# Attention, gated layer and cosine layer on one core: a planner that holds VectorE's and GpSimd's common port as a resource, and the last queries scaled by the step that reads their scores

## The chip, the cores and the metric

One core of a Trainium2 chip. The time is the device time of one execution in microseconds (us); three runs of the kernel before gave 1183.61, 1184.83 and 1186.10, median 1184.83. The engines are TensorE (PE, with PEld for its weight loads), VectorE (DVE), ScalarE (ACT), GpSimd (POOL) and SyncE (SP, which only issues transfers). Each runs its own list of instructions in order.

## The reference

For 4 batches x 8 heads x 576 tokens x 64, then two dense layers on the 2304 tokens:

```
scores = q @ k^T / 8;  thresh = max(scores) - tau
attn   = exp(scores - max) where scores >= thresh, else 0;  attn /= sum(attn)
x      = attn @ v                             # 2304 x 512
xn     = x / sqrt(mean(x*x) + 1e-6) * rms_g
x      = (silu(xn @ w_gate) * (xn @ w_val)) @ w_out       # 512 -> 1536 -> 512
h      = x @ w_in;  out = (h * cos(h)) @ w_out2           # 512 -> 2048 -> 512
```

## The kernel before

Attention works on 16 pairs of heads (4 batches x 4). The 576 queries of a pair make five score steps: four of 128 queries for both heads (`s`), and one (`s4`) that holds the last 64 queries of both heads. A score step writes one PSUM bank pair per head (`s0`, `s1`; `s4` writes only `s0`). For each step then: VectorE takes the maximum and copies the scores out of PSUM (`max`, L505), which frees the bank; ScalarE takes the exponential (`exp`, L523); GpSimd works out the threshold (`th`, L514); VectorE masks and sums (`mask`, L533); TensorE transposes the result (`t`, tile pst, L573, and the rest columns `c0`, `c1`, tile psc); ScalarE copies that out (`raw`). The two halves of a pair end in a product with v (`av0`, `av1`, tile po, L610), copied out by ScalarE (`avo`, L620). GpSimd divides the pair (`div`, L627), squares it (`sq`, L637) and adds it up over the batch (`x_add`, L641); at the batch's end TensorE sums over the partitions (`xsum`, tile pss, L650), and VectorE, GpSimd and SP turn that into the norm's factors in DRAM (`mean`, `rms`, `rs_out`).

The signs are turned: q is multiplied by -1/8 (`qscale`), so that the maximum becomes a minimum. For the 512 main queries ScalarE does it on its copy (L451). For the last 64 queries, tile q4, GpSimd does it in place before they are transposed (`scale_q4`, L424), 16 times.

The order of all this is written out by a planner (`Plan`). Every step has an engine, a cost and a place from the table `STEPS`: (engine, ns, place in ns, and for transfers the landing). `order()` plays the engines against each other: at each turn it takes the step that can start first, ties going to the lower place, and holds buffers, dependences, and a switch cost on TensorE. The result is only the order in which the instructions are written; on the chip the engines run by semaphores. `WARM_S` puts idle matmuls between the first score steps.

At the end of attention the planner also mixes in the first four units of the gated layer (`gv`, tile pgv, two halves of 12 matmuls each, on chunks 0 and 1 of the tokens). Behind the plan the dense layers run in a fixed order: first the second product of unit 0 (tile px), then the next gv.

The weights come as pairs of 32 bit words; VectorE, ScalarE and GpSimd turn them into floats and split these into a high and a low part (`j1`, `j2`, `j_a`, `j_p`, L281 to L300).

Of the kernel before, what the change touches and what calls it, by code (L numbers as in the profile page):

```python
# [14 lines left out]
ALU = mybir.AluOpType  # L15
# [10 lines left out]

UNIT = 3500
STEPS = {
    "none": ("", 0, 29644),
    "load_k": ("SP", 1700, -153470, 5000),  # L30
    "load_q": ("SP", 1700, 5248, 7000),
    "load_v": ("SP", 1700, 40101, 5000),
    "q4": ("POOL", 850, -97525),
    "pb": ("PE", 440, -11192),
    "pa": ("PE", 440, -25434),
    "pc": ("PE", 330, -13826),
    "pb_a": ("ACT", 590, 96411),
    "pa_a": ("ACT", 690, -507361),
    "pc_a": ("ACT", 480, 51091),
    "s": ("PE", 960, -101976),  # L40
    "s4": ("PE", 490, -10556),
    "warm": ("PE", 640, 138604),
    "max": ("DVE", 830, -168581),
    "exp": ("ACT", 785, 23446),
    "th": ("POOL", 450, -62469),
    "mask": ("DVE", 1040, 14956),
    "t": ("PE", 445, 36814),
    "raw": ("ACT", 595, -118822),
    "c0": ("PE", 220, -2475),
    "c1": ("PE", 440, -168991),  # L50
    "c_raw": ("ACT", 415, 220222),
    "radd": ("POOL", 300, 21216),
    "rinv": ("DVE", 400, -48222),
    "r_out": ("SP", 2100, -37205, 2500),
    "r_in": ("SP", 1700, -118771, 11000),
    "av0": ("PE", 2110, -332350),
    "av1": ("PE", 2660, -226081),
    "avo": ("ACT", 420, -105583),
    "div": ("POOL", 1420, 77077),
    "xout": ("SP", 500, -100632, 2500),  # L60
    "sq": ("POOL", 1200, -21513),
    "x_add": ("POOL", 1420, 100483),
    "xsum": ("PE", 1150, 59463),
    "mean": ("DVE", 150, -541635),
    "rms": ("POOL", 1330, 96684),
    "rs_out": ("SP", 2500, -200342, 2500),
    "x_load": ("SP", 500, 109454, 6000),
    "x_p": ("POOL", 1000, 80792),
    "x_a": ("ACT", 610, -82732),
    "x_d": ("DVE", 610, 41961),  # L70
    "jdma": ("SP", 500, 112560, 5000),
    "j1": ("DVE", 600, -13279),
    "j2": ("DVE", 690, -118552),
    "j_p": ("POOL", 1300, 206161),
    "j_a": ("ACT", 620, 63782),
    "gv": ("PE", 2100, 27390),
    "silu": ("ACT", 500, -78353),
    "hmul": ("DVE", 560, -166673),
    "hhi": ("ACT", 520, -75740),
    "hlo": ("DVE", 720, -172389),  # L80
}
SIGNAL = 100
SWITCH = 100
TILING = {"s": 1, "s4": 3, "av0": 2, "av1": 2}
WARM = (8, 2, 0, 0)
WARM_S = (3, 3, 3, 3, 3, 3)
# [9 lines left out]
class Plan:  # L96
# [19 lines left out]
    def order(self):  # L116
        steps, users = self.steps, dict(self.users)
        missing = [len(s["after"]) for s in steps]
        follow = [[] for _ in steps]
        for s in steps:  # L120
            for x in s["after"]:
                follow[x["n"]].append(s["n"])
        taken, parked = {tag: [] for tag in self.bufs}, {}
        ready = [0] * len(steps)
        freed = {}
        clock = {s["eng"]: 0 for s in steps}
        here = {eng: [] for eng in clock}
        for s in steps:
            if not s["after"]:
                here[s["eng"]].append(s["n"])  # L130
        out = []
        tiling = 0
        while len(out) < len(steps):
            best = None
            for eng, ns in here.items():
                for n in list(ns):
                    s = steps[n]
                    held = [taken[tag][-self.bufs[tag]] for tag, _ in s["take"]
                            if len(taken[tag]) >= self.bufs[tag]]
                    wait = [key for key in held if users.get(key, 1)]  # L140
                    if wait:
                        parked.setdefault(wait[0], []).append(n)
                        ns.remove(n)
                        continue
                    t = max([ready[n], clock[eng]] + [freed[key] for key in held])
                    if eng == "PE" and TILING.get(s["kind"], 0) != tiling:
                        t = max(t, clock[eng] + SWITCH)
                    if best is None or (t, s["place"], n) < best:
                        best = t, s["place"], n
            assert best, "no step can start"  # L150
            t, _, n = best
            s = steps[n]
            eng = s["eng"]
            if eng == "PE":
                tiling = TILING.get(s["kind"], 0)
            here[eng].remove(n)
            for tag, key in s["take"]:
                taken[tag].append(key)
            end = t + s["ns"]
            if eng:  # L160
                clock[eng] = end
            seen = end + s["landing"]
            for key in s["free"]:
                users[key] -= 1
                freed[key] = max(freed.get(key, 0), seen)
                if not users[key]:
                    for x in parked.pop(key, ()):
                        here[steps[x]["eng"]].append(x)
            for x in follow[n]:
                missing[x] -= 1  # L170
                ready[x] = max(ready[x], end if steps[x]["eng"] == eng != "SP" else seen)
                if not missing[x]:
                    here[steps[x]["eng"]].append(x)
            s["t"] = t
            out.append(s)
        return out

    def run(self):
        for s in self.order():
            s["fn"]()  # L180


@with_exitstack
def attention_moe_cos_kernel(
# [16 lines left out]
    nc = tc.nc  # L201
# [38 lines left out]
    qscale = const.tile([P, 1], F32, name="qscale")  # L240
# [96 lines left out]
    q4 = [acst.tile([P, P], F32, name=f"q4{i}") for i in range(2)]  # L337
# [21 lines left out]
    nat, qk, un, hf, pr, xb, rm, sq, pre = {}, {}, {}, {}, {}, {}, {}, {}, {}  # L359
# [60 lines left out]
    def k4_t(ps, p):  # L420
        nc.tensor.transpose(ps, nat["k", p][1].rearrange("p h d -> p (h d)"), ident)

    def scale_q4(p):
        nc.gpsimd.tensor_scalar(q4[p % 2][0:64], q4[p % 2][0:64], qscale[0:64, 0:1], None, op0=ALU.mult)  # L424

    def prep_pe(p, kind):


# [67 lines left out]
    def s_max(n, hd):  # L496

        g = group_of(n)
        if g not in grp:
            grp[g] = {"m": sm_p.tile([P, 5], F32, tag="m", name="m"), "n": 0}  # L500
        ci = grp[g]["n"]
        grp[g]["n"] += 1
        un[n]["ci", hd] = ci
        s = s_p.tile([P, S], F32, tag="s", name="s")
        nc.vector.tensor_scalar(  # L505
            s.rearrange("p (c n) -> p c n", c=2), un[n].pop(("ps", hd))[:, :, 0:288], 1.0, None,
            op0=ALU.mult, op1=ALU.min, accum_out=grp[g]["m"][:, ci:ci + 1],
        )
        un[n]["s", hd] = s
# [263 lines left out]
    def attention():  # L773
# [6 lines left out]
        add = plan.add  # L780
# [1 line left out]

        load_k(0)
        load_q(0)
        scale_q4(0)
        warm(WARM[0])
        for kind, m in zip("bac", WARM[1:]):
            prep_pe(0, kind)
# [4 lines left out]
        smm, mx, ex, mk, thr, sums, done = {}, {}, {}, {}, {}, {}, {}  # L793
        lk, lq, lv = {}, {}, {}
# [5 lines left out]
        for p in range(NPAIRS):  # L800
            n = 5 * p
            if p:
                lk[p] = add("load_k", n, load_k, p, take=[("kn", ("kn", p))])
                lq[p] = add("load_q", n, load_q, p, take=[("qn", ("qn", p)), ("q4", ("q4", p))]
                )
            lv[p] = add("load_v", n, load_v, p, take=[("vn", ("vn", p))])
            if p:
                z = add("q4", n, scale_q4, p, after=[lq.get(p)])
                last = []
                for kind, after, free in (  # L810
                    ("b", [lk.get(p)], [("kn", p)]),
                    ("a", [lq.get(p)], [("qn", p)]),
                    ("c", [lk.get(p), z], [("kn", p), ("q4", p)]),
                ):
                    nm = "q" if kind == "a" else "k"
                    x = add("p" + kind, n, prep_pe, p, kind, after=after + last, free=free,
                        take=[("t", ("pre", p, kind))]
                        + ([] if kind == "c" else [(nm, (nm, p))]),
                    )
                    last = [x]  # L820
                    ready[p].append(add("p" + kind + "_a", n, prep_act, p, kind, after=[x],
                        free=[("pre", p, kind)],
                    ))
        for n in range(NU):
            p, u = divmod(n, 5)
# [18 lines left out]
            if u == g[1][-1]:  # L844
                thr[g] = add("th", n, s_thr, g,
                    after=[mx[x] for x in mx if group_of(x[0]) == g],
# [11 lines left out]
        for j in range(2 * NPAIRS):  # L858
            p, par = divmod(j, 2)
# [124 lines left out]
        for n in range(N_EARLY):  # L984
            c = seq[n][1]
# [5 lines left out]
            x = add("hmul", NU + n, h_mul, n, after=[x, y], free=[("gv", n)])  # L991
            x = add("hhi", NU + n, h_hi, n, after=[x])
            hs.append(add("hlo", NU + n, h_lo, n, after=[x], free=[("hh", n)]))
        plan.run()

    with tc.manual_schedule():
        jobs += [
# [65 lines left out]
        done = 0  # L1063
# [178 lines left out]
```

## Time and profile before

| | |
|---|---|
| time, median of 3 runs | 1184.83 us (1183.61 to 1186.10) |
| the profiled execution | 1183.16 us, span 1181.4 us |
| granted TensorE clock | 0.999 of full |
| attention, with the first units of the gated layer | to 326 us of the span |
| gated layer | to about 780 us |
| cosine layer | to the end |
| busy over the span | PE 98%, DVE 69%, ACT 55%, POOL 29% |

The span runs from the first to the last instruction; 1.8 us of the time lie around it. The end of a matmul is modelled, so that a busy TensorE may still hold small waits; a step's true length is read from its start to the next one's start.

### The profile page before, as it was taken

What the parts mean: (1) busy time and instruction counts of PE and PEld (TensorE: products, weight loads), DVE (VectorE), ACT (ScalarE), POOL (GpSimd) and SP (SyncE); (2) the same over time, 40 slices, a digit from 0 to 9 for tenths busy, and PEclk for the clock granted to TensorE, in tenths of its full rate; (3) what the DMA queues carried; (4) which work ended last, traced back from release to release, by engine and by line L of the source; (5) the groups of instructions that cost most, each with busy time, mean ns of one, the idle gap of its engine ahead of it and who ended that gap; (6) DMA issues with size and microseconds to landing.
All of it is one profiled execution on the core that took longest, in us unless ns stands there. A gap on an engine that the chain in (4) does not pass through costs nothing.

```text
span 1181.4 us, 18229 instructions
## 1 busy us (share of the span) xinstructions
PE 1159.4 (98%) x6832; PEld 1017.9 (86%) x6832; DVE 820.8 (69%) x1571; ACT 647.2 (55%) x1210; POOL 342.3 (29%) x315
## 2 busy tenths in 40 slices
PE   8999999999999999999999999999999999999997
PEld 6666666666889999999999999999999999999995
DVE  5898888898659463644726429578687796867765
ACT  5887777877434221312313215377677676766663
POOL 2344444443744020110201102014234243332222
PEclk9999999999999999999999999999999999999999
DMA  5554323311452030110301102002112021000014
GB/s 123 131 132 112 100 58 78 95 48 46 151 175 76 32 108 1 54 54 1 107 1 50 59 1 83 25 1 72 37 36 72 1 72 36 23 15 1 1 54 108
DMA packets 99449, 71.67 MB, mean 61 GB/s; under 512 B 65040, under 2 KB 89360, under 8 KB 99360
## 3 DMA queue, kind: packets, MB, share of 16 engines
q1 hardware_dynamic: 98256, 70.20, 20.9%
q8 instruction: 54, 0.88, 0.3%
q10 hardware_dynamic: 1040, 0.26, 0.1%
q14 instruction: 35, 0.29, 0.1%
q0 software_dynamic: 64, 0.03, 0.0%
HBM read 60.95 MB, written 9.52 MB: 60 GB/s over the span
## 4 chain that ended last, share of the span: by engine, by line
PE 88%; DVE 3%; issue 3%; DMA 2%; ACT 2%; POOL 1%; SPq 0%; POOLq 0%; DVEq 0%; ACTq 0%
PE pgv L716 23%; PE ph L716 16%; PE po L716 16%; PE px L716 11%; PE s L485 7%; PE po L610 6%; PE pst L573 5%; PE psc L592 1%; PE psa L416 1%; DVE wtmp L286 1%; DVE s L505 1%; DMA raw<-in_moe_w_val_dram 1%; DVE e L533 0%; PE warm L682 0%; PE psb L416 0%
## 5 line engine op out<-in xcount | busy, mean ns | idle before, releaser
L290 POOL TENSOR_TENSOR wtmp<-wtmp,raw 128x512 int32<-128x512 int32 x68 | 96.1, 1413 | 353.3 <-DVE wtmp L286 345.2
L716 PE MATMUL pgv<-xh,whi 128*128 128x384 f32 x576 | 194.0, 337 | 0.0
L716 PE MATMUL pgv<-xl,whi 128*128 128x384 f32 x576 | 193.7, 336 | 0.0
L716 PE MATMUL pgv<-xh,wlo 128*128 128x384 f32 x576 | 193.5, 336 | 0.0
L1147 POOL TENSOR_TENSOR hlo<-r,hhi 128x384 fp32r<-128x384 f32 x96 | 98.0, 1021 | 304.0 <-ACT hhi L1146 248.0
L740 ACT ACTIVATE hh<-pgv 128x384 f32<-128x384 f32 x72 | 35.4, 492 | 254.2 <-PE pgv L716 254.1
L744 DVE TENSOR_TENSOR hh<-hh,pgv 128x384 f32<-128x384 f32 x72 | 39.7, 552 | 164.8 <-ACT hh L740 164.6
L505 DVE TENSOR_SCALAR_CACHE_REDUCE s<-s 128x576 f32<-128x576 f32 x144 | 103.8, 753 | 37.9 <-PE s L485 37.6
L716 PE MATMUL ph<-xh,whi 128*128 128x384 f32 x384 | 129.6, 337 | 0.0
L716 PE MATMUL ph<-xl,whi 128*128 128x384 f32 x384 | 129.5, 337 | 0.0
L716 PE MATMUL ph<-xh,wlo 128*128 128x384 f32 x384 | 129.2, 336 | 0.0
L533 DVE SCALAR_TENSOR_TENSOR e<-s,th,e 128x576 f32<-128x576 f32 x128 | 120.4, 971 | 0.4 <-POOL th L514 0.4
L1129 ACT ACTIVATE t<-ph,magic 128x384 f32<-128x384 f32 x96 | 55.8, 582 | 111.5 <-PE ph L716 111.5
L716 PE MATMUL po<-whi,hlo 128*128 128x512 f32 x288 | 114.5, 398 | 1.4 <-POOL hlo L1147 1.4
L716 PE MATMUL po<-whi,hhi 128*128 128x512 f32 x288 | 113.8, 395 | 0.2 <-ACT hhi L1146 0.2
L716 PE MATMUL po<-wlo,hhi 128*128 128x512 f32 x288 | 113.4, 394 | 0.0
L716 PEld LDWEIGHTS pgv<-xh,whi 128*128 128x128 f32 x576 | 108.2, 188 | 0.5 <-issue 0.5
L716 PEld LDWEIGHTS pgv<-xl,whi 128*128 128x128 f32 x576 | 108.2, 188 | 0.4 <-DVE xl L710 0.3
L716 PEld LDWEIGHTS pgv<-xh,wlo 128*128 128x128 f32 x576 | 108.2, 188 | 0.0
L523 ACT ACTIVATE e<-s,m 128x576 f32<-128x576 f32 x128 | 96.6, 781 | 12.5 <-DVE s L505 12.0
L716 PE MATMUL px<-hhi,whi 128*128 128x384 f32 x288 | 98.2, 341 | 4.0 <-DVE acc L1044 3.6
L1136 DVE SCALAR_TENSOR_TENSOR r<-t,r 128x384 f32<-128x384 f32 x96 | 99.1, 1032 | 3.3
(117 smaller groups left out, 2470.3 us busy)
## 6 DMA issues: line engine op xcount, KB each, us to landing
raw<-in_moe_w_out_dram SPq DMA_DIRECT2D x28, 512.0 KB
raw<-in_moe_w_in_dram SPq DMA_DIRECT2D x16, 512.0 KB
raw<-in_moe_w_gate_dram SPq DMA_DIRECT2D x12, 512.0 KB
raw<-in_moe_w_val_dram SPq DMA_DIRECT2D x12, 512.0 KB
x<-xb SPq DMA_DIRECT2D x16, 288.0 KB
kn<-in_k_dram SPq DMA_DIRECT2D x16, 256.0 KB
vn<-in_v_dram SPq DMA_DIRECT2D x16, 256.0 KB
qn<-in_q_dram SPq DMA_DIRECT2D x15, 256.0 KB
```

The costliest lines, as they stand in the source:

```text
L290: nc.gpsimd.tensor_tensor(tmp, tmp, lw, op=ALU.add)
L485: nc.tensor.matmul(ps[:, c, 0:288], lhs, kh[r, k0:k0 + 288], start=True, stop=True,)
L505: nc.vector.tensor_scalar(s.rearrange("p (c n) -> p c n", c=2), un[n].pop(("ps", hd))[:, :, 0:288], 1.0, None, op0=ALU.mult, op1=ALU.min, ...
L523: nc.scalar.activation(un[n]["e"][:, hd], un[n]["s", hd], AF.Exp, bias=grp[group_of(n)]["m"][:, c], scale=-1.0)
L533: nc.vector.scalar_tensor_tensor(e, un[n].pop(("s", hd)), grp[group_of(n)]["th"][:, ci:ci + 1], e, op0=ALU.is_le, op1=ALU.mult, accum_out= ...
L573: nc.tensor.transpose(ps[:, c], e[:, hd, k0:k0 + P], ident)
L610: nc.tensor.matmul(po[64 * hd:64 * hd + 64, :], vn[:, c, hd, :] if c < 4 else vl[:, hd, :], hf[j]["et"][:, hd, c, :] if c < 4 else hf[j][" ...
L716: nc.tensor.matmul(ps, w[a], x[bb], start=first and i == 0, stop=last and i == 2)
L744: nc.vector.tensor_tensor(hq[n], hq[n], pgv.pop(n)[:, 1, 0:TC], op=ALU.mult)
L1129: nc.scalar.activation(t, ph, AF.Identity, bias=magic[:, 0:1], scale=INV2PI)
L1136: nc.vector.scalar_tensor_tensor(r, t, -C2, r, op0=ALU.mult, op1=ALU.add)
L1147: nc.gpsimd.tensor_tensor(lo, r, f(hi), op=ALU.subtract)
```

## The change

The table gets other costs and other places for every step. The planner gets a set `LOCK` of step kinds of VectorE and GpSimd that use the port: none of them starts in the plan while another of them runs, whichever of the two engines it is on. `BEHIND`, the kinds that would also get a real wait for VectorE's step, is empty, so that no wait is written. `scale_q4` is gone, and the maximum of an `s4` step multiplies by `qscale` instead of 1.0.

```diff
-    "q4": ("POOL", 850, -97525),
-    "s": ("PE", 960, -101976),
-    "s4": ("PE", 490, -10556),
+    "s": ("PE", 960, -21325),
+    "s4": ("PE", 490, 85459),
...
-    "th": ("POOL", 450, -62469),
-    "mask": ("DVE", 1040, 14956),
+    "th": ("POOL", 300, -18608),
+    "mask": ("DVE", 890, -37373),
...
-    "av1": ("PE", 2660, -226081),
+    "av1": ("PE", 2660, -60188),
...
+LOCK = {
+    "mask", "j1", "j2", "x_d", "hlo", "th", "div", "sq", "x_add", "rms", "radd", "x_p", "j_p",
+}
+BEHIND = set()
...
+                    if s["kind"] in LOCK:
+                        t = max(t, port)
...
+            if s["kind"] in LOCK:
+                port = end
+                if eng == "DVE":
+                    holder = s
+                elif s["kind"] in BEHIND:
+                    s["behind"] = holder
...
-    def scale_q4(p):
-        nc.gpsimd.tensor_scalar(q4[p % 2][0:64], q4[p % 2][0:64], qscale[0:64, 0:1], None, op0=ALU.mult)
...
-            s.rearrange("p (c n) -> p c n", c=2), un[n].pop(("ps", hd))[:, :, 0:288], 1.0, None,
+            s.rearrange("p (c n) -> p c n", c=2), un[n].pop(("ps", hd))[:, :, 0:288],
+            qscale[:, 0:1] if n % 5 == 4 else 1.0, None,
...
-            if p:
-                z = add("q4", n, scale_q4, p, after=[lq.get(p)])
...
-                    ("c", [lk.get(p), z], [("kn", p), ("q4", p)]),
+                    ("c", [lk.get(p), lq.get(p)], [("kn", p), ("q4", p)]),
```

**Place 1: TensorE at the end of attention.** Before, the last two products with v (po) of the last pair are followed by gated-layer matmuls (pgv); these are the last rows of po:

```order
L573 MATMUL pst<-ident,el 128x128 x4
L610 MATMUL po<-et,vn 64x256 x8
L610 MATMUL po<-ec,v_96 64x256 x2
L610 MATMUL po<-et,vn 64x320 x8
L610 MATMUL po<-ec,v_96 64x320 x2
L716 MATMUL pgv<-xh,whi 128x384
```

Between them and the sum over the partitions (pss) stand four halves of pgv, 48 matmuls. Now the last rows before the second product (px) of the gated layer are these:

```order
L736 MATMUL pgv<-xl,whi 128x384
L736 MATMUL pgv<-xh,wlo 128x384
L630 MATMUL po<-et,vn 64x320 x8
L630 MATMUL po<-ec,v_96 64x320 x2
L670 MATMUL pss<-ones,sq 128x1 x5
L736 MATMUL px_4139<-hhi,whi 128x384
```

All eight halves of pgv have moved ahead of the last po, and pss stands directly behind it.

**Place 2: TensorE around the last queries' score step of the twelfth pair** (s with `64x288` is s4, s with `128x288` a full step). Before:

```order
L573 MATMUL pst<-ident,e 128x128 x4
L416 MATMUL psa<-ident,qn 128x128 x4
L573 MATMUL pst<-ident,e 128x128 x4
L485 MATMUL s_2891<-k 64x288 x4
L416 MATMUL psc<-ident,kn 128x128
L421 MATMUL psc<-ident,k_2382 128x128
```

Now:

```order
L617 MATMUL psc<-ident,el 64x128
L593 MATMUL pst<-ident,el 128x128 x4
L593 MATMUL pst<-ident,e 128x128 x4
L504 MATMUL s_2913<-k 64x288 x4
L504 MATMUL s_2927<-k,q 128x288
L504 MATMUL s_2928<-k,q 128x288
```

The next full score step has moved directly behind s4. In the whole order a score step stands directly behind a score step in five places now and in three before.

**Place 3: VectorE at the end of attention.** Before, from the maximum of the last pair's s4 on (s,m is max; e and el with sum are masks, el of an s4 step):

```order
L505 TENSOR_SCALAR s,m<-s_3788 128x576
L533 SCALAR_TENSOR_TENSOR e,sum<-s,th,e 128x576 x4
L533 SCALAR_TENSOR_TENSOR el,sum<-s,th,el 128x576
L545 RECIPROCAL r_147<-r_147 128x9
L546 STREAM_TRANSPOSE rt<-r_147 128x32
```

Now:

```order
L524 TENSOR_SCALAR s,m<-s_3716,qscale 128x576
L553 SCALAR_TENSOR_TENSOR e,sum<-s,th,e 128x576 x8
L565 RECIPROCAL r_146<-r_146 128x9
L566 STREAM_TRANSPOSE rt<-r_146 128x32
L730 SCALAR_TENSOR_TENSOR xl<-x_2526,g_sb,xh 128x384
L553 SCALAR_TENSOR_TENSOR el,sum<-s,th,el 128x576
```

Nine masks of the last pair, not five, are left when its last scores have been read.

## Rows read from the trace of the kernel before

**Rows 1.** The page, part 1: busy time and share by engine.

```profile
PE 1159.4 (98%) x6832; PEld 1017.9 (86%) x6832; DVE 820.8 (69%) x1571; ACT 647.2 (55%) x1210; POOL 342.3 (29%) x315
```

**Rows 2.** Busy time in stretches: length, engines, PEclk, DMA share, GB/s.

```profile
20.00:300.00 280.00, 273.99 (x2051) 182.03 (x2050) 242.74 (x607) 216.92 (x394) 124.90 (x126) 1.00 0.34 90
300.00:326.00 26.00, 25.50 (x171) 22.70 (x170) 15.51 (x23) 12.47 (x26) 18.73 (x17) 1.00 0.45 144
326.00:400.00 74.00, 70.02 (x396) 68.38 (x396) 49.05 (x85) 26.15 (x51) 24.74 (x13) 1.00 0.36 113
400.00:780.00 380.00, 379.59 (x2164) 378.73 (x2163) 201.94 (x360) 110.48 (x216) 40.34 (x31) 1.00 0.14 42
```

**Rows 3.** Waits from 20 to 300 us: total us, times, longest us.

```profile
DVE s L505 <- PE s L485: 31.9, 42, 1.7
...
PE s L485 <- DVE s L505: 3.6, 7, 0.9
```

**Rows 4.** Timeline of TensorE, four score steps: start, us, idle before.

```profile
51.87 0.70 PE L485 MATMUL s<-k 64*64 64x288 f32 x4 [0.85 <-DVE s L505]
...
187.07 0.70 PE L485 MATMUL s<-k 64*64 64x288 f32 x4 [0.27 <-DVE s L505]
...
205.54 1.19 PE L485 MATMUL s<-k 64*64 64x288 f32 x8 [0.85 <-DVE s L505]
...
260.34 1.24 PE L485 MATMUL s<-k,q 64*128 64x288 f32 x8 [0.87 <-DVE s L505]
```

**Rows 5.** Timeline of VectorE at 204 us, two maxima and what follows.

```profile
204.72 0.76 DVE L505 TENSOR_SCALAR_CACHE_REDUCE s<-s 128x576 f32<-128x576 f32 x1 [0.58 <-PE s L485]
...
205.40 0.76 DVE L505 TENSOR_SCALAR_CACHE_REDUCE s<-s 128x576 f32<-128x576 f32 x1
```

**Rows 6.** Costliest groups of GpSimd and VectorE up to 326 and 300 us.

```profile
L424 POOL TENSOR_SCALAR q<-q,qscale 64x128 f32<-64x128 f32 x16 | 12.6, 789 | 5.6 <-DMA q<-in_q_dram 3.6 <-PE pst L573 1.8
...
L533 DVE SCALAR_TENSOR_TENSOR e<-s,th,e 128x576 f32<-128x576 f32 x123 | 116.5, 977 | 0.0
```

**Rows 7.** The chain in order of time, transpositions at 301 us: start, us, what.

```profile
301.10 1.31 PE pst L573 x12
```

**Rows 8.** Timeline of VectorE, two masks at 295 us.

```profile
295.19 0.82 DVE L533 SCALAR_TENSOR_TENSOR e<-s,th,e 128x576 f32<-128x576 f32 x1
...
295.93 1.95 DVE L533 SCALAR_TENSOR_TENSOR e<-s,th,e 128x576 f32<-128x576 f32 x1
```

**Rows 9.** Timeline of GpSimd: a division beside those masks, and the last pair's chain.

```profile
295.40 1.87 POOL L627 TENSOR_TENSOR xb<-t,rb 128x576 f32<-128x576 f32 x1
...
317.99 1.43 POOL L627 TENSOR_TENSOR xb<-t,rb 128x576 f32<-128x576 f32 x1
319.49 1.15 POOL L637 TENSOR_TENSOR sq<-xb 128x576 f32<-128x576 f32 x1
320.72 1.44 POOL L641 TENSOR_TENSOR sq<-sq 128x576 f32<-128x576 f32 x1
```

**Rows 10.** Timeline of TensorE from the last po to the first px.

```profile
313.27 2.37 PE L610 MATMUL po<-et,vn 128*64 128x320 f32 x16 [0.50 <-ACT t L620]
315.48 0.71 PE L610 MATMUL po<-ec,v 128*64 128x320 f32 x4
316.12 0.44 PE L716 MATMUL pgv<-xh,whi 128*128 128x384 f32 x1
...
324.54 1.17 PE L650 MATMUL pss<-ones,sq 128*128 128x1 f32 x10
325.57 0.42 PE L716 MATMUL px<-hhi,whi 128*128 128x384 f32 x1
```

**Rows 11.** Timeline of ScalarE: the last pair's copy out of po.

```profile
316.23 0.43 ACT L620 COPY t<-po 128x320 f32<-128x320 f32 x1 [3.01 <-PE po L610]
```

**Rows 12.** Waits from 300 to 400 us.

```profile
PE px L716 <- DVE acc L1044: 3.6, 3, 1.7
```

More of the change, by code (lines that the diff above doesn't have):

```diff
@@ L28 @@
 STEPS = {
[L29 to L32, printed above, removed]
-    "q4": ("POOL", 850, -97525),
[L34 to L39, printed above, removed]
-    "s": ("PE", 960, -101976),
-    "s4": ("PE", 490, -10556),
-    "warm": ("PE", 640, 138604),
-    "max": ("DVE", 830, -168581),
@@ L44 @@
-    "exp": ("ACT", 785, 23446),
-    "th": ("POOL", 450, -62469),
-    "mask": ("DVE", 1040, 14956),
[L47 to L56, printed above, removed]
-    "av1": ("PE", 2660, -226081),
-    "avo": ("ACT", 420, -105583),
@@ L59 @@
[L59 to L80, printed above, removed]
+    "none": ("", 0, 27559),
+    "load_k": ("SP", 1700, -172962, 5000),
+    "load_q": ("SP", 1700, -46102, 7000),
+    "load_v": ("SP", 1700, -4761, 5000),
+    "pb": ("PE", 440, -19143),
+    "pa": ("PE", 440, -15661),
+    "pc": ("PE", 330, -8379),
@@ new lines @@
+    "pb_a": ("ACT", 590, 81106),
+    "pa_a": ("ACT", 690, -473960),
+    "pc_a": ("ACT", 480, 49428),
+    "s": ("PE", 960, -21325),
+    "s4": ("PE", 490, 85459),
+    "warm": ("PE", 640, 37404),
+    "max": ("DVE", 833, -172383),
+    "exp": ("ACT", 785, 72251),
+    "th": ("POOL", 300, -18608),
+    "mask": ("DVE", 890, -37373),
+    "t": ("PE", 438, 31564),
+    "raw": ("ACT", 595, -92045),
+    "c0": ("PE", 220, -3639),
+    "c1": ("PE", 440, -315186),
+    "c_raw": ("ACT", 415, 218185),
@@ new lines @@
+    "radd": ("POOL", 250, 94231),
+    "rinv": ("DVE", 430, -4519),
+    "r_out": ("SP", 2100, -108544, 2500),
+    "r_in": ("SP", 1700, -320774, 11000),
+    "av0": ("PE", 2110, -371909),
+    "av1": ("PE", 2660, -60188),
+    "avo": ("ACT", 420, 4517),
+    "div": ("POOL", 1410, 8372),
+    "xout": ("SP", 500, -179658, 2500),
+    "sq": ("POOL", 1145, 63241),
+    "x_add": ("POOL", 1410, 86580),
+    "xsum": ("PE", 1150, 399585),
+    "mean": ("DVE", 150, -681609),
+    "rms": ("POOL", 1520, 138440),
@@ new lines @@
+    "rs_out": ("SP", 2500, -32428, 2500),
+    "x_load": ("SP", 500, 48239, 6000),
+    "x_p": ("POOL", 1010, 169405),
+    "x_a": ("ACT", 610, -116593),
+    "x_d": ("DVE", 550, 94630),
+    "jdma": ("SP", 500, 52341, 5000),
+    "j1": ("DVE", 600, -115045),
+    "j2": ("DVE", 690, -98093),
+    "j_p": ("POOL", 1310, 466908),
+    "j_a": ("ACT", 620, 67088),
+    "gv": ("PE", 2100, 18969),
+    "silu": ("ACT", 500, -124840),
+    "hmul": ("DVE", 560, -259566),
+    "hhi": ("ACT", 520, -319947),
@@ L81 @@
+    "hlo": ("DVE", 560, -244125),
 }
@@ L131, in order @@
         out = []
-        tiling = 0
+        tiling, port, holder = 0, 0, None
         while len(out) < len(steps):
@@ L176, in order, with run @@
         return out
-    def run(self):
+    def run(self, tc):
+        done = tc.nc.cur_bb.bb.instructions
+        wait = mybir.DependencyInfo(mybir.DependencyClass.Sync, mybir.DependencyReason.DATA)
         for s in self.order():
+            n = len(done)
             s["fn"]()
+            if s["eng"] == "DVE" and s["kind"] in LOCK:
+                s["ins"] = done[-1]
+            if s.get("behind"):
+                for x in done[n:]:
+                    tc.add_manual_dep(x, s["behind"]["ins"].name, wait, reason="port")
 @with_exitstack
@@ L784, in attention @@
         load_q(0)
-        scale_q4(0)
         warm(WARM[0])
@@ L993, in attention @@
             hs.append(add("hlo", NU + n, h_lo, n, after=[x], free=[("hh", n)]))
-        plan.run()
+        plan.run(tc)
     with tc.manual_schedule():
```

## The prediction

> **What bounds the kernel now.** I read the page's busy shares first: TensorE is busy for 1159.4 of 1181.4 us [rows 1], so any change must show as TensorE standing still more or less, or as other work for it. Then the busy times by stretch [rows 2]: from 400 to 780 us TensorE is idle for 0.4 us of 380, and the change doesn't touch that code. What it can reach is attention with the first units of the gated layer. There TensorE is idle for 6.0 us of 280 between 20 and 300 us, 0.5 us of 26 up to 326 us, and 4.0 us of 74 behind it. VectorE is the next busiest, 242.7 of 280 us, but it follows: its maxima wait 31.9 us in total for the score steps, while TensorE's score steps wait 3.6 us for the maxima [rows 3]. So in attention a us is won or lost only where TensorE waits, and the question is how many such waits the new order has. At full clock throughout (PEclk 1.00 in these rows) no step changes its speed.
>
> **TensorE's work stays.** No matmul is added or removed; the steps are the same 376 of attention, the eight gv halves among them. The order changes between full-width, score and v-product steps 175 times against 173, which at some 0.1 us each is 0.2 us: I count nothing. So the end of attention moves by the difference of the waits alone.
>
> **Term 1, score steps behind score steps.** A score step needs the bank that the maximum before it frees. Where s4 and s stand directly behind each other, TensorE waits: 0.85 us at 51.87, 0.85 at 205.54 and 0.87 at 260.34 [rows 4], 2.57 together. That is one maximum: its successor starts 0.68 us behind it [rows 5], and the rest is signalling. The new order has four places where s directly follows s4, at one maximum each (0.85), and one where a full step directly follows a full step of both heads, which must wait for two maxima: 2 x 0.68 + 0.17 = 1.53. Together 4.9 us against 2.6, so +2.3 us. In two more places only one transposition, or one with the short c0 step, stands between a full step and the next full step. Two maxima and signalling are 1.53, and the gap holds 0.6 to 0.9 us of work, so 0.9 and 0.6 us are left; before, the one place with a single transposition between waited 0.27 [rows 4]. That is +1.2 us. The waits are not fully additive, since a standing TensorE lets VectorE catch up at the next place; I take +3 us for this term, with 0 and +4 as its ends.
>
> **Term 2, the last masks.** Place 3 of the order leaves nine masks of the last pair behind its last maximum, five before. TensorE transposes four tiles in 1.31/3 = 0.44 us [rows 7]; VectorE makes a mask every 0.74 us where it is alone (295.19 to 295.93) [rows 8]. Behind s4 stand five transpositions, of which the third to fifth need the first three of these masks: the first is ready 0.68 + 0.74 + 0.15 = 1.57 us after s4 and wanted after 0.97, and each further one falls back by 0.3. So the fifth starts 1.2 us late. The v product behind them (2.84 us) lets VectorE get ahead again. +1.2 us, between 0 and +3.3: where a GpSimd operation meets a mask, the mask took 1.95 instead of 0.82 [rows 8, 9], 1.1 us more, and up to three such operations can fall there.
>
> **Term 3, the last pair's sum.** Before, four gv halves (316.12 to 324.54, 8.4 us) stood between the last v product and pss [rows 10], and hid copy, division, square and sum. Now pss is directly behind the v product in TensorE's list, and behind pss waits everything else. The v product ends at 316.12; the copy starts 0.11 us later and takes 0.43 [rows 11]; the three GpSimd operations take 1.43, 1.15 and 1.44 [rows 9], and with the signals of about 0.06 between them the sum is 0.11 + 0.43 + 4.02 + 0.2 = 4.76 us in which TensorE has nothing. What is saved is the 0.50 us that the last v product waited for the copy of its bank [rows 10]. So +4.2 us. The division needs the pair's factors from DRAM; with eight gv halves (17 us) ahead of the v product they are there. The lower end is +3.5, the upper +6, where the low halves of the next chunk on VectorE fall on the three operations. What follows pss hangs on pss as before: the norm's factors, the loads behind them on SP's queue, and the 4.0 us of waits up to 400 us, of which 3.6 are px behind the copies of its own banks [rows 12]. I leave them as they are, give or take 1 us.
>
> **Term 4, the scaling that goes.** 16 operations of 789 ns, 12.6 us of GpSimd [rows 6]. GpSimd is busy for 125 of 280 us [rows 2] and nothing in TensorE's waits names it. Where they fell on a mask they held it up: at most 12.6 us of VectorE's time, most of it inside VectorE's own 31.9 us of waiting. I take -0.5 us, with -3 and 0 as ends. The maximum with a scale per row instead of 1.0 is the same instruction with another operand, 16 of 144; no row shows this form. The nearest is the maximum itself (0.76); I take no change. If it were 0.1 us longer, 1.6 us of VectorE would lie in the same cover. Moved loads: no wait of TensorE in this stretch is for a transfer long enough to matter, so nothing.
>
> **The port.** The trace has masks of 0.82 us alone and of 1.95 beside a division of 1.87 us, which takes 1.43 alone [rows 8, 9]; the mean mask is 0.98 [rows 6]. So the collisions are real, and cost VectorE some 0.16 x 123 = 20 us in attention. The plan now spaces such steps, but nothing is written that makes an engine wait, and VectorE on the chip runs ahead of or behind the plan. The Trainium skill ("SBUF — State Buffer", section "Who interferes with whom") says that the second of the two is blocked for the whole instruction when a VectorE operation has two SBUF inputs and GpSimd reads SBUF. The trace agrees as far as one pair shows it: the mask that starts 0.53 us into the division would end 1.34 + 0.74 = 2.08 us later by the rule, and took 1.95. By the rule each of the 16 scalings that goes can give back its 0.79 us; this is the first rival's mechanism.
>
> **Sum.** 3 + 1.2 + 4.2 - 0.5 = 7.9, say +8 us. On the profiled execution that is 1183.2 + 8 = 1191.2 us (span 1181.4 + 8 = 1189.4, with the same 1.8 us around it); its time lies 1.7 us under the median of three, so the forecast for a median is 1184.8 + 8 = 1192.8.
>
> **The rivals.** First, VectorE paces attention and the port is what holds it: then the 12.6 us of scalings come off, the score steps' places cost nothing extra, and only the 4.2 us at the end are paid: 1184.8 - 12.6 + 4.2 = 1176.4. For it speaks that masks lose 20 us to collisions; against it that VectorE waits 31.9 us for scores. It decides once VectorE's maxima no longer wait for TensorE. Since TensorE's idle time is only 6.0 us, more than that can't come out of waits that show; the rest would have to be hidden in its modelled ends. Chance 0.10.
> Second, the other places and costs close the old waits, the 3.4 us that have nothing to do with adjacent scores too, and VectorE is ahead enough that the new ones don't open: -6.0 + 4.2 = -1.8, so 1183.0, no change by a measurement of this kernel, which tells 0.2% (2.4 us). For it speaks that the costs of mask and th in the table are nearer to the trace; against it that s4 still stands at 490 ns where TensorE's steps of it take 1.1 [rows 4], so that the plan believes TensorE earlier than it is. Chance 0.14.
> Third, the end is worse than I count: three GpSimd operations on the last nine masks (+3.3 instead of part of 1.2) and VectorE's low halves of the next chunk late for the third gv unit, another 2 us: 1184.8 + 8 + 2.1 + 2 = 1197. Chance 0.12.
> The forecast itself 0.64.
>
> **From these the numbers.** Slower by over 0.2%: 0.64 + 0.12 = 0.76; within: 0.14; faster: 0.10. The range goes down to 1184, which holds part of the second rival (term 1 at 0, term 4 at -3, term 3 at 3.5), and up to 1198; the forecast's own range is 1188 to 1196.
>
> **What would show it.** In the profile after, pss has an idle time of 4 to 5 us before it, released by GpSimd's sum. TensorE's waits for L524 between 20 and 300 us rise from 3.6 to 6 or 7 us, the five adjacent score steps among them. The fifth transposition behind the last s4 waits for a mask. TensorE from 400 us on takes as long as before. It would be wrong if pss starts less than 322 us into the span, if TensorE's idle time between 20 and 300 us falls under 4 us, or if the waits between pss and 400 us shrink by more than 2.

## The result, and the profile after

The changed kernel takes 1193.42 us in the median of four runs (1192.38 to 1195.16), the kernel before 1185.46 beside it: a ratio of 1.0074, with a 95% interval of 1.0057 to 1.0091. It is slower, by 8.0 us; 1192.8 was forecast, with slower at 0.76. The profiled execution took 1194.08 us, its span is 1192.3.

The stretches of [rows 2], moved with the work, read now (length, then PE, PEld, DVE, ACT, POOL busy with their instructions, PEclk, DMA share, GB/s):

```profile
0.00:20.00 20.00, 16.68 (x94) 12.70 (x94) 7.96 (x37) 8.52 (x13) 2.38 (x9) 0.91 0.64 129
20.00:300.00 280.00, 272.42 (x2039) 182.36 (x2039) 233.15 (x603) 216.91 (x393) 112.81 (x113) 1.00 0.35 91
300.00:334.00 34.00, 29.11 (x185) 24.29 (x181) 15.07 (x30) 13.93 (x27) 15.62 (x14) 0.95 0.36 108
334.00:408.00 74.00, 70.43 (x387) 68.85 (x387) 47.49 (x82) 24.57 (x47) 26.05 (x15) 0.96 0.36 113
408.00:788.00 380.00, 379.93 (x2168) 379.61 (x2167) 200.07 (x357) 108.49 (x212) 39.33 (x30) 1.00 0.14 42
```

From 408 us on nothing differs by more than 0.4 us. The loss is at the end of attention: TensorE idles for 4.9 us of the 34 before 334 us, and PEclk is no longer 1.00 there nor right behind. TensorE's timeline at this place (start, us, idle time before) answers to [rows 10]:

```profile
325.68 2.37 PE L630 MATMUL po<-et,vn 128*64 128x320 f32 x16
327.88 0.71 PE L630 MATMUL po<-ec,v 128*64 128x320 f32 x4
333.49 2.29 PE L670 MATMUL pss<-ones,sq 128*128 128x1 f32 x10 [4.89 <-POOL sq L661]
335.64 0.67 PE L736 MATMUL px<-hhi,whi 128*128 128x384 f32 x1
```

GpSimd's chain that it waits for, against [rows 9], and the granted clock in the stretches behind it:

```profile
329.14 1.40 POOL L647 TENSOR_TENSOR xb<-t,rb 128x576 f32<-128x576 f32 x1 [9.92 <-ACT t L640]
330.62 1.34 POOL L657 TENSOR_TENSOR sq<-xb 128x576 f32<-128x576 f32 x1
332.04 1.40 POOL L661 TENSOR_TENSOR sq<-sq 128x576 f32<-128x576 f32 x1
```

```profile
333.00:335.00 2.00, 1.51 (x8) 1.52 (x8) 0.00 (x0) 0.58 (x1) 2.00 (x3) 0.50 0.00 0
335.00:339.00 4.00, 4.00 (x15) 4.00 (x16) 1.43 (x4) 0.65 (x2) 3.28 (x3) 0.50 0.00 0
```

PEclk 0.50 is TensorE's lower level, 1.2 instead of 2.4 GHz, right behind a stretch in which it did nothing. pss takes 2.15 us from its start to px instead of 1.03, and px with it 3.84 from its start to the next gv instead of 2.17: 1.1 and 1.7 us that the prediction did not have.

The score steps directly behind score steps wait as the count of the order said, five times (against [rows 4]); the rows at 159.71 and 213.67 are the two places with only a transposition, or one and the short c0 step, between:

```profile
35.84 1.91 PE L504 MATMUL s<-k,q 64*128 64x288 f32 x8 [0.85 <-DVE s L524]
...
76.04 1.24 PE L504 MATMUL s<-k,q 64*128 64x288 f32 x8 [0.93 <-DVE s L524]
...
159.71 1.91 PE L504 MATMUL s<-k,q 64*128 64x288 f32 x8
...
169.65 1.24 PE L504 MATMUL s<-k,q 64*128 64x288 f32 x8 [0.93 <-DVE s L524]
...
213.67 1.91 PE L504 MATMUL s<-k,q 64*128 64x288 f32 x8 [0.26 <-DVE s L524]
...
227.25 1.24 PE L504 MATMUL s<-k,q 64*128 64x288 f32 x8 [0.93 <-DVE s L524]
...
244.24 1.24 PE L504 MATMUL s<-k,q 64*128 64x288 f32 x8 [0.93 <-DVE s L524]
```

The number in brackets is not the whole wait. Three of these rows take 1.91 us instead of 1.24: the matmuls of their second head start one maximum later than those of the first, and this second wait lies inside the row, where TensorE counts as busy. It is 0.67 us each time, so that 35.84 loses 1.52 us, 213.67 loses 0.93 and 159.71 loses 0.7.

But attention as a whole has not got longer. From 20 to 280 us, the stretch ahead of the last masks, before and after:

```profile
20.00:280.00 260.00, 254.01 (x1906) 168.63 (x1906) 226.07 (x565) 203.13 (x369) 118.53 (x120) 1.00 0.35 92
```

```profile
20.00:280.00 260.00, 254.33 (x1911) 170.95 (x1911) 215.48 (x560) 202.94 (x368) 102.88 (x104) 1.00 0.35 91
```

TensorE is idle for 6.0 us before and 5.7 after. Of this idle time, the waits for the maxima rise from 3.6 to 5.2 us, and all others fall from 2.4 to 0.5; VectorE has 10.6 us less to do. Two groups of VectorE, before and then after (up to 300 us; mean ns behind the bar), say where from:

```profile
L286 DVE SCALAR_TENSOR_TENSOR wtmp<-raw,wtmp 128x512 int32<-128x512 int32 x6 | 7.5, 1250 | 0.2
```

```profile
L553 DVE SCALAR_TENSOR_TENSOR e<-s,th,e 128x576 f32<-128x576 f32 x122 | 109.4, 930 | 0.1
...
L308 DVE SCALAR_TENSOR_TENSOR wtmp<-raw,wtmp 128x512 int32<-128x512 int32 x6 | 4.1, 691 | 0.1
```

The mask's mean went from 977 ns [rows 6] to 930, that of a weight step from 1250 to 691: the operations that meet on the port collide less on the chip too, though nothing makes them wait. Not all of this is the port's place in the plan. With the scalings alone gone (e3 below) the two means are 961 and 1054, and with the new table but no port in the plan (e6 below) 951 and 831.

At the last masks, TensorE's and VectorE's timelines, with GpSimd's beside them:

```profile
295.56 1.37 PE L593 MATMUL pst<-ident,e 128*128 128x128 f32 x8 [0.74 <-ACT et L603]
297.93 0.72 PE L593 MATMUL pst<-ident,e 128*128 128x128 f32 x4 [0.99 <-DVE e L553]
298.57 3.93 PE L630 MATMUL po<-et,vn 128*64 128x320 f32 x16
```

```profile
294.60 0.81 DVE L553 SCALAR_TENSOR_TENSOR e<-s,th,e 128x576 f32<-128x576 f32 x1
...
295.33 0.82 DVE L553 SCALAR_TENSOR_TENSOR e<-s,th,e 128x576 f32<-128x576 f32 x1
...
296.08 1.69 DVE L553 SCALAR_TENSOR_TENSOR e<-s,th,e 128x576 f32<-128x576 f32 x1
...
297.70 1.95 DVE L553 SCALAR_TENSOR_TENSOR e<-s,th,e 128x576 f32<-128x576 f32 x1
```

```profile
295.55 1.61 POOL L657 TENSOR_TENSOR sq<-xb 128x576 f32<-128x576 f32 x1
297.23 1.80 POOL L661 TENSOR_TENSOR sq<-sq 128x576 f32<-128x576 f32 x1
```

Two of the masks run beside a square and a sum and take twice as long. The transpositions wait 0.74, 0.11 and 0.99 us, for the masks of 294.60, 295.33 and 296.08 in turn, of which only the third is a long one. (The first row names ScalarE's copy as the releaser; in the profiles of e1, e4 and e7, with the same steps up to there, it is the mask.)

A landmark makes this addable. From the start of the third score step to pss TensorE has the same steps in both orders: 324.54 - 13.99 = 310.55 us before, 333.49 - 15.24 = 318.25 after, +7.7. Of that, 4.89 - 0.50 is the wait at pss, 1.84 the masks, 1.56 the v product at 298.57, which ran at a low clock in this profile (3.93 us instead of 2.37; PEclk 0.57 from 298 to 302 us), and -0.3 the stretch to 280 us; 0.2 are left over. The v product stands right behind the masks' waits, but the profiles of e1, e4 and e5 below have the same waits there and 1.00, so that this fall came in one profile of four. The third score step itself starts 1.25 us later; that is the start of the program, and the experiments show that it is not the change's.

### The profile page after: what moved, and what is told of

It is laid out like the page before. It is cut to its first block, busy times and chain, and to the rows that moved or that the text cites. A ratio compares the mean times of both kernels' runs of the same rounds, so it can differ in the third digit from the quotient of the medians.

```text
span 1192.3 us, 18193 instructions
## 1 busy us (share of the span) xinstructions
PE 1165.4 (98%) x6832; PEld 1023.2 (86%) x6832; DVE 809.3 (68%) x1571; ACT 647.6 (54%) x1210; POOL 327.2 (27%) x299
## 4 chain that ended last, share of the span: by engine, by line
PE 90%; issue 3%; DVE 3%; ACT 1%; POOL 1%; DMA 1%; SPq 0%; POOLq 0%; DVEq 0%; ACTq 0%
PE pgv L736 23%; PE ph L736 16%; PE po L736 16%; PE px L736 11%; PE s L504 8%; PE po L630 7%; PE pst L593 5%; PE psc L612 1%; DVE e L553 1%; PE psa L438 1%; DMA raw<-in_moe_w_out_dram 0%; DVE wtmp L308 0%; PE warm L702 0%; PE psb L438 0%; DVE hlo L772 0%
## 5 line engine op out<-in xcount | busy, mean ns | idle before, releaser
L524 DVE TENSOR_SCALAR_CACHE_REDUCE s<-s 128x576 f32<-128x576 f32 x128 | 91.8, 753 | 38.7 <-PE s L504 38.6
L553 DVE SCALAR_TENSOR_TENSOR e<-s,th,e 128x576 f32<-128x576 f32 x128 | 114.0, 925 | 0.5 <-POOL th L534 0.5
```

Source lines behind the costliest of these rows:

```text
L524: nc.vector.tensor_scalar(s.rearrange("p (c n) -> p c n", c=2), un[n].pop(("ps", hd))[:, :, 0:288], qscale[:, 0:1] if n % 5 == 4 else 1.0, ...
L553: nc.vector.scalar_tensor_tensor(e, un[n].pop(("s", hd)), grp[group_of(n)]["th"][:, ci:ci + 1], e, op0=ALU.is_le, op1=ALU.mult, accum_out= ...
```

## The experiments

Two theories went in. A: the loss sits at the end, in the wait before pss and in the clock behind it. B: it is spread over the score steps. The kernel before ran beside each; its medians there were 1184.5 to 1184.8, and the ratios are to these.

**One dependence puts four halves of gv back between the v product and pss (e1, then e5).**

```diff
-            x = add("gv", NU + n, gv_mm, n, 0, after=(x0, x1)[c] + jops + [smm[NU - 1], g1],
+            last_av = [outs[2 * NPAIRS - 1]["after"][0]] if n >= 2 else []
+            x = add("gv", NU + n, gv_mm, n, 0, after=(x0, x1)[c] + jops + [smm[NU - 1], g1] + last_av,
                 take=[(f"s{1 - n % 2}", ("gv", n))],
```

> The changed kernel, with one dependence more in the plan: the third unit of gv waits for the last product with v, so that four halves of gv stand between that product and pss again, as in the kernel before. Theory A (the loss sits at the end: 4.9 us of waiting before pss, and 2.8 us that pss and the first px lost at half the clock behind that wait): both go, 1193.4 - 7.7 = 1185.7 us, no wait over 1 us before pss, PEclk 1.00 behind it. Rival B (the loss is spread over the score steps that stand behind each other, and the wait before pss only uncovers time that would be lost later): under 2 us come back, 1191.5 to 1193.5. Rival C (the wait goes but TensorE then waits for the last masks or for the factors from DRAM instead): 1188 to 1190.

Measured: 1190.32 us (ratio to before 1.0048, 1.0035 to 1.0060). The wait before pss is gone and PEclk behind it is 1.00, but only 3.1 us came back: theory A's number failed. The time is just above C's range, and as in C the wait has moved, though to a place that C did not name. Right behind px the gv waits (TensorE's timeline):

```profile
333.00 0.44 PE L736 MATMUL pgv<-xh,whi 128*128 128x384 f32 x1 [0.86 <-ACT xh L726]
336.14 0.45 PE L736 MATMUL pgv<-xl,whi 128*128 128x384 f32 x1 [2.71 <-DVE xl L730]
```

In this plan GpSimd's last scaling of chunk 2 had moved behind the norm's power, and its low half ran on VectorE beside the 3.4 us scaling of chunk 3, 3.11 us long. The clock falls here too: PEclk is 0.50 from 338 to 340 us, and the work from the first gv behind px to the last matmul takes 851.9 us instead of 847.0, which is more than the two waits. One more dependence repairs that (e5):

```diff
+        done["rs", B - 1]["after"][0]["after"][0]["after"] += [y["after"][0]["after"][0] for y in x2]
```

> As e1_after_tail, and besides the norm's power (rms) of the last batch waits in the plan for GpSimd's scalings of chunk 2, so that these stand ahead of it again, as before the change. In e1 the last of them stood behind it, and TensorE waited 0.86 and 2.71 us for that chunk's low halves. Theory A: these 3.6 us go too: 1190.3 - 3.6 = 1186.7 us (1185.5 to 1188), what is left over the kernel before being the late masks (2.4 us) less what the score steps' part gained (1.8). Rival E (GpSimd's chain is too long for four halves of gv in any order): the wait shows again before pss or px, and the time stays at 1189 to 1191.

Measured: 1186.20 us (1.0014, 1.0005 to 1.0024), as A said. Both waits are gone. Between the medians 7.2 us are back; against the kernel before beside each, 1.4 of the 8.0 us are left. The landmark's stretch is 311.61 us, 1.06 more than before: the masks' 1.84, less the 0.50 that the last v product no longer waits, leave -0.3 for the rest of it, as above.

**The other way round: the kernel before with its last v product put behind all eight halves of gv (e2).**

```diff
             y = add("gv", NU + n, gv_mm, n, 1, after=[x])
+            if n == N_EARLY - 1:
+                outs[2 * NPAIRS - 1]["after"][0]["after"].append(y)
```

> The kernel before, with the last product with v put behind all eight halves of gv, directly in front of pss, as the change does; nothing else. Theory A: a wait of 4.5 to 5 us before pss, and half the clock for pss and the first px behind it (2.8 us): 1184.8 + 4.3 + 2.8 = 1191.9 us, that is +6.5 to +7.5. If only the wait counts and the clock fell by chance in the one profile of the changed kernel: +4.2, 1189. Rival B: under +2.

Measured: 1192.71 us (1.0072, 1.0059 to 1.0084), +8.2, a little over the span that was given. This one place makes the kernel before as slow as the changed one. TensorE's timeline:

```profile
330.45 2.29 PE L650 MATMUL pss<-ones,sq 128*128 128x1 f32 x10 [5.21 <-POOL sq L641]
332.61 0.67 PE L716 MATMUL px<-hhi,whi 128*128 128x384 f32 x1
```

and its granted clock behind the wait:

```profile
330.00:336.00 6.00, 5.55 (x21) 5.55 (x22) 0.38 (x2) 0.00 (x0) 1.58 (x2) 0.50 0.01 3
```

So the clock's fall belongs to the wait and not to one unlucky profile.

**The wait filled with idle matmuls (e4):** in the changed kernel, 22 of them ahead of pss.

```diff
         ss = sq.pop(b * NP)
+        if b == B - 1:
+            warm(22)
```

> The changed kernel, with 22 idle matmuls (about 4.8 us) between the last product with v and pss, in the place of the wait. The wait for GpSimd's sum stays, so pss starts at the same time. If TensorE's clock falls because it stands still there, pss and the first px now run at full clock and 2.8 us come back: 1193.4 - 2.8 = 1190.6. If the fall has another cause, PEclk is 0.5 behind pss as before and the time stays at 1193.4.

Measured: 1189.55 us (1.0048, 1.0034 to 1.0062), 3.9 less than the changed kernel against 2.8 expected. The timeline and the clock:

```profile
325.81 5.18 PE L704 MATMUL warm<-ones 128*128 128x128 f32 x44
330.82 1.23 PE L672 MATMUL pss<-ones,sq 128*128 128x1 f32 x10
331.91 0.42 PE L738 MATMUL px<-hhi,whi 128*128 128x384 f32 x1
```

```profile
320.00:340.00 20.00, 20.00 (x139) 18.25 (x138) 5.84 (x10) 5.09 (x10) 11.01 (x7) 1.00 0.19 65
```

pss waits as long as before, but it and px run at full clock. TensorE's standing still is what takes the clock down, and 2.8 us of the loss is that. The other 1.1 us of this difference are within the spread that the start of the program brings (below).

**The scaling alone (e3).** The order of the kernel before word for word; GpSimd's scalings are left out and the maximum of s4 scales.

```diff
     def scale_q4(p):
-        nc.gpsimd.tensor_scalar(q4[p % 2][0:64], q4[p % 2][0:64], qscale[0:64, 0:1], None, op0=ALU.mult)
+        pass
...
-            s.rearrange("p (c n) -> p c n", c=2), un[n].pop(("ps", hd))[:, :, 0:288], 1.0, None,
+            s.rearrange("p (c n) -> p c n", c=2), un[n].pop(("ps", hd))[:, :, 0:288],
+            qscale[:, 0:1] if n % 5 == 4 else 1.0, None,
```

> The kernel before with its order kept word for word, but GpSimd's 16 scalings of the last queries are left out and the maximum of an s4 step multiplies by the scale. Theory A (VectorE is not the bound; the scalings lie beside its waits): -0.5 us, between -2 and +0.5. Rival D (GpSimd's 12.6 us and the port hold VectorE, and through it TensorE): -3 us or more, with less idle time of TensorE between 20 and 280 us. The maximum takes 0.82 instead of 0.75 us in these 16.

Measured: 1183.86 us (0.9996, 0.9987 to 1.0004): no change that can be told, and D's 3 us are outside the interval. GpSimd is busy for 106.3 us from 20 to 280 instead of 118.5, VectorE for 225.2 instead of 226.1. The 12.2 us of GpSimd were worth 0.9 of VectorE and nothing sure to the kernel.

**The table without the port (e6).**

```diff
-LOCK = {
-    "mask", "j1", "j2", "x_d", "hlo", "th", "div", "sq", "x_add", "rms", "radd", "x_p", "j_p",
-}
+LOCK = set()
```

> The changed kernel with an empty LOCK, that is its table of costs and places, played without the port. Its order has four halves of gv between the last v product and pss, and nine score steps or so directly behind others, where the changed kernel has five. Theory A: no wait before pss (-4.4 - 2.8 against the changed kernel), but by the same count as in the prediction some 8 us more of waits between score steps: 1192 to 1196. Rival F (the port in the plan is what costs, the table alone is good): under 1187.

Measured: 1201.74 us (1.0140, 1.0126 to 1.0154). F is out: the port in the plan is not the cost, without it this table is 8.3 us worse. A's size was too small, and its reason only part of it. The waits for the maxima, as far as they show, are 7.0 us up to 300 us against 5.2, but TensorE idles for 9.9 us from 20 to 280, not 5.7, and the longest wait is for a mask, not for a maximum:

```profile
178.55 0.33 PE L610 MATMUL psc<-ident,e 128*128 128x128 f32 x1 [2.50 <-DVE e L551]
```

It also has the late low halves of e1, 0.82 and 2.71 us before the next gv. From its third score step to pss it takes 322.0 us, with no wait at pss: 11.5 more than the kernel before, of which the idle time shows only a part. What this does not settle is what the port would be worth with places of its own for a plan without it; that was not tried.

**The last masks without GpSimd beside them (e7).** As e5, and the square and sum of the third last pair wait in the plan for the scalings of chunk 1:

```diff
+        late_sq = next(s for s in plan.steps if s["kind"] == "sq" and s["at"] == 5 * (NPAIRS - 3) + 4)
+        late_sq["after"] += [y["after"][0]["after"][0] for y in x1]
```

> As e5_after_tail2, and besides GpSimd's square and sum of the third last pair wait in the plan for the scalings of chunk 1, so that they no longer run beside the last pair's masks. In the changed kernel two of these masks took 1.69 and 1.95 us instead of 0.81, and TensorE waited 0.74 and 0.99 us for them. Theory A: about 1.7 us less than e5: 1185 (1183 to 1186.5). Rival G (the masks are too many anyway, as the prediction counted: 1.2 us even without GpSimd): 0.5 us less than e5 at most.

Measured: 1184.43 us (0.9998, 0.9989 to 1.0007), 1.8 less than e5. The same masks on VectorE:

```profile
296.14 0.81 DVE L553 SCALAR_TENSOR_TENSOR e<-s,th,e 128x576 f32<-128x576 f32 x1
...
296.88 0.81 DVE L553 SCALAR_TENSOR_TENSOR e<-s,th,e 128x576 f32<-128x576 f32 x1
```

The waits behind s4 are 0.74, 0.11 and 0.11 us, 0.96 together instead of 1.84: the 0.74, which the expectation put on GpSimd too, is still there. The landmark's stretch shows half of the 1.8, 310.71 us instead of 311.61; what the other half is, no profile shows (e5's runs spread from 1183.99 to 1187.99, those of e7 from 1184.17 to 1185.51). So the masks' wait was about half their number and half their meeting with GpSimd.

**The start (e8 and e9).** In the profile after and in those of e1, e2, e3, e5, e6 and e7 the matmuls soon behind the wait for the keys are slow; in those of before and e4 they are not. First e5, then e8, which has five idle matmuls more there (TensorE's timeline):

```profile
6.69 0.45 PE L443 MATMUL psb<-ident,k 128*128 128x128 f32 x1 [1.88 <-DMA k<-in_k_dram]
...
9.28 0.42 PE L438 MATMUL psc<-ident,kn 128*128 128x128 f32 x1
```

```profile
6.77 0.30 PE L443 MATMUL psb<-ident,k 128*128 128x128 f32 x1 [0.44 <-DMA k<-in_k_dram]
...
8.12 0.27 PE L438 MATMUL psc<-ident,kn 128*128 128x128 f32 x1
```

```diff
-WARM = (8, 2, 0, 0)
+WARM = (13, 2, 0, 0)
```

> As e7_best, with 13 idle matmuls instead of 8 ahead of the first keys, so that TensorE doesn't stand still for 2 us before them. In four of six profiles of the kernels so far the first matmuls behind that stand ran at half the clock (0.42 us a transposition instead of 0.27), which put the second score step 1.1 us later. Theory H (the stand brings that): about 0.7 us less than e7_best in the median and first transpositions of 0.27 us. If the clock there goes by chance alone: as e7_best within 0.3 us.

> The kernel before with 13 idle matmuls instead of 8 ahead of the first keys, nothing else. e8_best_warm stands 1.8 us under the kernel before, of which e7_best has 0.4. Theory H (the idle matmuls keep the clock for the first steps, in any order of the rest): -1 to -1.8 us here too, 1183 to 1184, so that the change, mended, is worth no more than 0.4 us. If they help only the mended kernel: 1184.5 to 1185.

Measured: e8, the mended change with it, 1183.02 us (0.9986, 0.9977 to 0.9994); e9, the kernel before with it and nothing else, 1182.91 (0.9987, 0.9978 to 0.9996). H holds for both, by 1.4 and 1.6 us. e8 beats both kernels, by 1.8 us and 10.4; but what makes it faster than the kernel before are the idle matmuls at the start, and e9 has them without any of the change. The runs of e8 lie between 1182.92 and 1183.21, ten of the eleven of e9 between 1182.61 and 1183.05 with one at 1183.58, those of the kernel before between 1182.93 and 1186.60: most of the spread from run to run was this start.

## Why the prediction was right, and where not

- **Term 3, the wait at pss (+4.2): right.** 4.89 - 0.50 = 4.4, by the chain of copy, division, square and sum that was added up; e2 and e5 show it from both sides.
- **What was missing: the clock behind the wait, 2.8 us.** The prediction took the full clock of attention as given, "so no step changes its speed". Behind a wait of 4.9 us it was 0.50; e4 shows that the standing still brings this, since the full clock comes back with the wait in place.
- **Term 1, score steps behind score steps (+3): every place came as counted, but the step from them to the whole failed.** The five adjacent places lost 0.93 us four times and 1.52 once, 5.2 together against 4.9 counted, and the two near ones 0.7 and 0.93 against 0.6 and 0.9; that is about 4.0 us more than the places of before (2.57 and 0.27). The sign that was given, 6 or 7 us of waits for the maxima, shows as 5.2 us of idle time, with 2.0 more inside the three long rows. The assumption that the rest of the stretch stays was wrong: it gave some 4.3 us back, so that the stretch is 0.3 us better, below the term's lower end. Of these, 1.9 are the waits for other things than maxima, 2.4 before and 0.5 after; the others are not split further here; waits inside other rows are among them (before, a score step at 104.73 us took 1.91 us too). The count of adjacent steps sees only these places; the second rival had the old waits closing, and was right in that half.
- **Term 2, the last masks (+1.2): right in place, small.** 1.84 us, of which e7 gives 0.88 to GpSimd beside one mask; the range went to 3.3 for that reason. Without it the masks' number alone costs 0.96.
- **Term 4, the scalings (-0.5): right.** -0.65 between medians, not to be told from none; the first rival's 12.6 us are excluded. The maximum with a scale per row takes 0.82 instead of 0.75 us.
- **The sum was right by two errors that cancel:** -3.3 in term 1 and +2.8 of clock. That 8.0 us were measured where 7.9 were added up is luck. The profiled spans differ by more, 10.9 us, since 1.25 us of start and 1.56 of the v product at a low clock fell on the profile after and not on that of before; e1, e4 and e5 don't have the second.
- Behind pss TensorE waits 3.6 us in the next 74 (4.0 before), as left.

## What to carry to other kernels

When a planner's new order is read, look first at the last link of each chain that leaves the planned part: a product that is moved to the end costs nothing in the plan's middle and the whole of its chain where nothing is left to cover it. A wait on TensorE can cost more than itself: here the work behind waits of 4.9 and 5.2 us ran at the lower clock, and idle matmuls in the wait brought that part back. A count of one kind of wait in an order says where these waits come, not what the sum does: check it against the whole stretch, from the start of one known step to the start of another, since a wait inside a row doesn't show as idle time.

## What the runs showed of the hardware

- After about 5 us of standing still TensorE's granted clock was 0.50 for the next 5 us or so (333 to 339 us after, 330 to 336 in e2); with idle matmuls in that gap it stayed at 1.00 (e4). Shorter waits did it too, but not each time: behind the 2.71 us of e1 it was 0.50 (338 to 340 us), behind the masks' 1.84 us it fell in one profile of four.
- At the start, after 1.9 to 2.2 us of waiting for the keys, the transpositions soon behind it (psc) took 0.42 us in seven of nine profiles and 0.27 in two, kernels and orders mixed. In e5 PEclk reads 1.00 in that stretch all the same (in the profile after, 0.55 from 8 to 10 us); only the length of the matmuls tells. With the gap cut to 0.44 us (e8) they took 0.27.
- A mask that started while a GpSimd operation was running took up to 1.95 us instead of 0.81 (296.08 and 297.70 us after, 295.93 before). Most masks were not lengthened: the median is 0.81 in both orders. GpSimd's operation grows as well: the square of 295.55 us, which started 0.22 us into a mask, took 1.61 us instead of the 1.15 of [rows 9].
